# Attention and gated FFN on one core: batch 0 in two token halves, rows of h turned by copies, loads unpaced, targets set anew

## The chip, the cores and the metric

The kernel runs on one core of one Trainium2 chip. The metric is the device time of one execution in microseconds, as the median of several runs; lower is better. The engines are TensorE (PE, with its weight loads as PEld), VectorE (DVE), ScalarE (ACT), GpSimd (POOL) and SyncE (SP), which here only issues DMAs.

## The reference

Eight batches of 576 tokens go through windowed attention (8 heads of 64, window of 32 to each side) and then through a feed-forward layer that is gated by a convolution over three tokens:

```python
scores = scale * np.matmul(q, k.transpose(0, 1, 3, 2))          # q, k, v: (8, 8, 576, 64)
scores = np.where(np.abs(pos[:, None] - pos[None, :]) <= 32, scores, -1e9)
attn = softmax(scores)                                          # + 1e-9 in the denominator
x = np.matmul(attn, v)             # heads side by side: (8, 576, 512)
h = np.maximum(x @ w_in, 0.0)      # (8, 576, 1024)
conv_out = sum(conv_w[k] * hp[:, k:k + S, :] for k in range(3))  # hp: h with a zero row at each end
gate = 1.0 / (1.0 + np.exp(-conv_out))
out = (h * gate) @ w_out           # (8, 576, 512), float32
```

## The kernel before, in words

**A planner writes the order.** The kernel first describes its work as tasks in `Order.add`: the engines that may run the task with a modelled duration (`act`, `dve`, `pl`, `pe`, `dma`), what it reads and writes, the PSUM banks that it opens, and a target `t`. `Order.run` is a list scheduler at build time: of the tasks that are ready on an engine it takes the one with the smallest target, a task that ACT or DVE may do goes to the one that would be done first, and DMAs are modelled as one channel with so many packets of so many ns. The result is a fixed program order on each engine. The targets come from `PARAMS`. All instructions are issued through one helper, so they all carry line 274 in the profile; the trace is read by tiles.

**Attention, for each batch.** `loads` issues on SP four loads of q and k (two head groups; `qst`, `kst`) and five blocks of v (`vst`; 128 tokens with an offset of 32), all float32; POOL casts them to bf16 (`qb`, `kb`, `ve`), and DVE makes `vo`, the blocks of v shifted by 64 partitions. One staging buffer exists for each, and two sets of the cast tiles. `transposes` turns q and k on PE (`qT`, `kT`), `scores` computes 64 x 128 blocks around the diagonal, ACT takes the exponential into `attn`, DVE multiplies by the mask, `values` multiplies by v (with a column of ones for the sum), DVE normalises into `xn`, and `x_turned` turns that into `xT`.

**FFN, in chunks of 384 tokens.** Two batches make three chunks (c 0 to 11). `first` multiplies by `w_in` for each of eight blocks m of 128 rows of h and applies relu into `hT`. `gates` does the convolution on PE by small diagonal matrices of 32 x 32; block m's result comes out turned by 32 x (m mod 4) partitions, so that four matmuls use different parts of the array. Hence h itself has to be turned too, for six of the eight blocks: `moves` does this by DMAs on SP from `hT` to `gT`, two for each shift `s_`. ACT takes a tanh into `tn`, DVE forms the product in place in `gT` (with `hT` directly for the blocks that aren't turned), and `second` multiplies by `w_out`, whose rows were loaded turned to match. ACT or DVE copies the result to `wst`, and SP stores it. c 1 is done in two parts, since its first half needs only batch 0.

**Order at the start.** SP's order is batch 0's q, k and v, then w_in, batch 1's loads, w_out, then the moves, later loads and stores as the planner has them. From batch 2 on, `paced` makes each load wait for the load before the last. As SP works in order, a DMA that waits for its source holds those behind it.

Of the kernel before, what the change touches and what calls it, by code (L numbers as in the profile page):

```python
# [31 lines left out]
class Order:  # L32
# [3 lines left out]
    def __init__(self):  # L36
        self.tasks, self.writer, self.readers = [], {}, {}

    def add(self, kinds, emit, t, reads=(), writes=(), opens=None, ps=(), after=(), claims=()):


        deps = set(after)
        soft = set()
        for k in claims:
            soft.update(self.readers.get(k, ()))
        for k in reads:
            if k in self.writer:
                deps.add(self.writer[k])
        for k in writes:
            if k in self.writer:  # L50
                deps.add(self.writer[k])
            deps.update(self.readers.get(k, ()))
        task = Task(len(self.tasks), kinds, emit, t, deps, opens, ps)
        task.soft = soft - deps
        for k in reads:
            self.readers.setdefault(k, []).append(task)
        for k in writes:
            self.writer[k] = task
            self.readers[k] = []
        for p in ps:  # L60
            p.readers += 1
        self.tasks.append(task)
        return task
# [131 lines left out]
def kernel(  # L195
# [53 lines left out]
    hT_pp = [sb([128, MB, CH + (4 if i == 1 else 2)], BF16, f"hT{i}") for i in range(3)]  # L249
# [98 lines left out]

    def loads(b):
        i = b % NLD  # L350

        def load_qk(y, j):
# [4 lines left out]
            )  # L357

# [21 lines left out]
        if b < 2:  # L380
            x, dx = (-100.0 if b == 0 else -50.0), 0.1
        else:
            x, dx = t0 - PARAMS["LD"], Q["LX"]
# [3 lines left out]
        def paced():  # L387
            return before[-2:-1] if b > 1 and len(before) > 1 else []

        for j in range(NPH):  # L390
            for y in range(2):
                t = x + n * dx
                o.add({"SP": dma(256, 110)}, lambda e, y=y, j=j: load_qk(y, j), t,
                      writes=[("st", y, j)], after=paced())
                before.append(o.tasks[-1])
                o.add({"POOL": pl(1152)}, lambda e, y=y, j=j: cast_qk(y, j, e), t,
                      reads=[("st", y, j)], writes=[("b", i, y, j)])
                n += 1
        for c in range(NBLK):
            t = x + n * dx  # L400
            o.add({"SP": dma(1024, 21)}, lambda e, c=c: load_v(c), t, writes=[("vst", c)], after=paced())
            before.append(o.tasks[-1])
            o.add({"POOL": pl(512)}, lambda e, c=c: cast_v(c, e), t,
                  reads=[("vst", c)], writes=[("ve", i, c)])
            n += 1
        for cs in ((0, 2), (2, 4)) if b == 0 else ((0, 4),):
            for half in range(2):
                o.add({"DVE": dve(520 * (cs[1] - cs[0]), 4)},
                      lambda e, cs=cs, half=half: shift(half, cs), x + n * dx,
                      reads=[("ve", i, c + half) for c in range(*cs)],  # L410
                      writes=[("vo", i, c, half) for c in range(*cs)])

    def load_w_in():
        for h in range(2):
# [9 lines left out]
            o.add({"SP": dma(512, 95)}, load, -60.0, writes=[("ws", 4 * h + c) for c in range(4)])  # L424
            for c in range(KC):
                o.add({"POOL": pl(512)}, lambda e, h=h, c=c: cast(e, h, c), -60.0 + h,
                      reads=[("ws", 4 * h + c)], writes=[("w_in", h, c)])

    def load_w_out():
        rows = moe_w_out.rearrange("(h c p) f -> p h c f", c=4, p=128)  # L430
        for c in range(4):
            def load(e, c=c):
                for lo, at, n in turn(c):
# [5 lines left out]
            o.add({"SP": dma(256, 95, len(turn(c)))}, load, -40.0,  # L439
                  writes=[("ws", 4 * h + c) for h in range(2)])  # L440
            for h in range(2):
                o.add({"POOL": pl(512)}, lambda e, h=h, c=c: copy(e, w_out_sb[:, 4 * h + c, :], ws[:, 4 * h + c, :]),
# [18 lines left out]
    def conv_weights():  # L461
        ps = Banks(1)
        o.add({"PE": pe(200.0, "f32")},
              lambda e: tensor.matmul(bank(ps, 0)[:, 0:3 * MB], conv_w24, ident24, start=True, stop=True),
              5.0, opens=ps, writes=[("cw24",)])
        o.add({"DVE": dve(24)}, lambda e: vector.tensor_copy(
            out=conv_w_sb.rearrange("p k m -> p (k m)"), in_=bank(ps, 0)[:, 0:3 * MB]),
            5.0, reads=[("cw24",)], writes=[("cw",)], ps=[ps])
        o.add({"DVE": dve(768)}, lambda e: vector.tensor_tensor(
# [5 lines left out]
    def transposes(g2):  # L475
# [3 lines left out]
        i, n = b % NLD, g2 % NKT  # L479
        for y in range(2):  # L480
# [16 lines left out]
            o.add({"PE": pe(280.0, "rows")}, mm, t + Q["TR"],  # L497
                  reads=[("b", i, y, j)], writes=[("tr", g2, y)], opens=ps,
                  claims=[("T", n, y, h) for h in range(2)])
            for h in range(2):  # L500
                o.add({"ACT": act(576), "DVE": dve(576)},
                      lambda e, ps=ps, h=h, to=to: copy(
                          e, to[:, h, :, :], half(ps, h).rearrange("p (j x) -> p x j", x=64)),
                      t + Q["TC"], reads=[("tr", g2, y)], writes=[("T", n, y, h)], ps=[ps])
# [4 lines left out]
    def scores(g):  # L509
# [3 lines left out]
        for part, ts in enumerate((range(0, 5), range(5, 9))):  # L513
            ps = Banks(2, 2)
            w = 64 * len(ts)

            def mm(e, ps=ps, ts=ts):
                for x in ts:
# [8 lines left out]
            o.add({"PE": pe(28.0 * len(ts), "rows")}, mm, t + Q["SC"] * d,  # L527
                  reads=[("T", n, y_, y) for y_ in range(2)],
                  writes=[("sc", g, part)], opens=ps, claims=[("a", a, part)])
            o.add({"ACT": act(2 * w)},  # L530
# [3 lines left out]
                  t + Q["EX"] * d, reads=[("sc", g, part)], writes=[("a", a, part)], ps=[ps])  # L534
        o.add({"DVE": (850.0, 850.0, None)},
# [3 lines left out]
    def values(g):  # L539
# [5 lines left out]
        ps = Banks(2, 2)  # L545

        def mm(e):
            for h in range(2):
                for c in range(NBLK):
                    for j in range(2):  # L550
                        x = min(2 * c + j, NT - 1)
                        tensor.matmul(
                            bank(ps, h)[64 * j:64 * j + 64, 65 * c:65 * c + 65],
# [6 lines left out]
        o.add({"PE": pe(29.0 * 10, "cols")}, mm, t + Q["AV"] * d,  # L560
              reads=[("a", a, 0), ("a", a, 1)] + [("ve", i, c) for c in range(NBLK)]
              + [("vo", i, c, h) for c in range(NBLK - 1) for h in range(2)],
              writes=[("av", g)], opens=ps, claims=[("xn", b % 2, pr), ("rec", a)])

        def po():
            return pair(ps, 0)[:, :, 0:65 * NBLK].rearrange("p e (c x) -> p e c x", x=65)

        o.add({"DVE": dve(70)}, lambda e: vector.reciprocal(rec, po()[:, :, :, 64]), t + Q["AX"] * d,
              reads=[("av", g)], writes=[("rec", a)], ps=[ps])
        h0 = head(pr, 0)  # L570
        o.add({"DVE": dve(640)},
              lambda e: vector.tensor_tensor(
                  out=xn_pp[b % 2][:, :, h0:h0 + 3:2, :].rearrange("p c e d -> p e c d"),
                  in0=po()[:, :, :, 0:64],
                  in1=rec[:, :, :, None].broadcast_to([128, 2, NBLK, 64]), op=ALU.mult),
              t + Q["AX"] * d, reads=[("av", g), ("rec", a)], writes=[("xn", b % 2, pr)], ps=[ps])

    def x_turned(b, c, n):

        t, d = pair_t[b * NP + NP - 1]  # L580
        t = t + Q["XT"] * d + 0.1 * c
# [7 lines left out]
        def mm(e):  # L589
            for i in range(n):  # L590
# [7 lines left out]
        o.add({"PE": pe(4 * n * (cols / 2.4 + 3))}, mm, t,  # L598
              reads=[("xn", b % 2, i) for i in range(NP)], writes=[("xps", b, c)], opens=ps,
              claims=[("xT", b // 2 % 2, b % 2, c + i) for i in range(n)])  # L600
        o.add({"ACT": act(4 * n * cols), "DVE": dve(4 * n * cols)},
# [4 lines left out]
              writes=[("xT", b // 2 % 2, b % 2, c + i) for i in range(n)], ps=[ps])  # L606


    def span(c, part):
# [3 lines left out]
        return (lo, hi) if part is None else ((lo, lo + HW + 1), (hi - HW - 1, hi))[part]  # L613

    def first(c, m, part, t):
# [19 lines left out]
        def relu(e):  # L635
# [10 lines left out]
            else:  # L646
                o0 = 1 if kind == 0 else 0
# [3 lines left out]
            else:  # L651
# [3 lines left out]
        o.add({"PE": pe(4 * (n / 2.4 + 3))}, mm, t,  # L655
              reads=need + [("w_in", m // 4, i) for i in range(KC)], writes=[("ph", c, m, part)], opens=ps,
              claims=[("h", kind, m, p_) for p_ in ((0, 1) if part is None else (part,))])
        o.add({"ACT": act(n), "DVE": dve(n)}, relu, t + Q["RL"], reads=[("ph", c, m, part)],
              writes=[("h", kind, m, p_) for p_ in ((0, 1) if part is None else (part,))], ps=[ps])
# [28 lines left out]
    def moves(c, qds, part, t):  # L688
        kind, halves, n, taps, gate = views(c, part)
        for s_ in range(1, 4):  # L690
            ms = [4 * qd + s_ for qd in qds]

            def move(e, m=ms[0], s_=s_):
                for lo, to, cnt in turn(s_):
                    if len(qds) > 1:
                        sync.dma_start(gate(m, to, to + cnt, 2, 4), taps(m, 1, lo, lo + cnt, 2))
                    else:
                        sync.dma_start(gate(m, to, to + cnt), taps(m, 1, lo, lo + cnt))

            runs = 2 if kind == 1 and part is None else 1  # L700
            o.add({"SP": dma(128 * runs * len(qds), 46 if n > HW and runs == 1 else 28, 2, PARAMS["MV"])},
                  move, t, reads=[("h", kind, m, p_) for m in ms for p_ in halves],
                  writes=[("g", c % 3, m, p_) for m in ms for p_ in halves])

    def gates(c, qd, part, t, late):
# [7 lines left out]
        def mm(e):  # L713
            for kk in range(3):
# [8 lines left out]
        o.add({"PE": pe(3 * (n / 2.4) + 100.0, "conv")}, mm, t,  # L723
              reads=[("h", kind, m, p_) for m in ms for p_ in halves] + [("diag",)],
              writes=[("pc", c, qd, part)], opens=ps,
              claims=[("tn", tn_i, u) for u in range(2)])
        for u in range(2):
            o.add({"ACT": act(2 * n)},
                  lambda e, u=u: scalar.activation(
                      tn[:, 2 * u:2 * u + 2, 0:n], pair(ps, 2 * u)[:, :, 0:n], AF.Tanh, bias=0.0, scale=1.0),  # L730
                  t + Q["TN"], reads=[("pc", c, qd, part)], writes=[("tn", tn_i, u)], ps=[ps])
        for m0, count, us in ((0, 1, (0,)), (1, 1, (0,)), (2, 2, (1,))):
            m = 4 * qd + m0
            ii = [("h", kind, m, p_) for p_ in halves] if m0 == 0 else []

            def product(e, m=m, m0=m0, count=count):
# [4 lines left out]
                else:  # L741
# [4 lines left out]
            o.add({"DVE": dve(n * count)}, product, late,  # L746
                  reads=[("tn", tn_i, u) for u in us] + ii,
                  writes=[("g", c % 3, m + x, p_) for x in range(count) for p_ in halves])
# [9 lines left out]
    def second(c, i, t):  # L758
# [4 lines left out]
        def mm(e):  # L763
            for m in range(MB):
# [6 lines left out]
        o.add({"PE": pe(8 * 216.0)}, mm, t,  # L771
              reads=[("g", c % 3, m, p_) for m in range(MB) for p_ in halves]
              + [("w_out", m) for m in range(MB)], writes=[("py", c, i)], opens=ps, claims=[("ws", n)])
# [94 lines left out]
```

## Time and profile before

| what | value |
|---|---|
| median of 3 runs | 242.4 us (242.24 to 243.18) |
| profiled execution | 243.37 us, span from first to last instruction 241.7 us |
| PE busy | 208.1 us (86%) |
| DVE, ACT, POOL busy | 160.1, 164.0, 80.9 us |
| DMA queue of SP | 67152 packets, 49.03 MB, 71.6% of 16 engines |
| mean granted TensorE clock | 0.972 |
| moves of h (gT from hT) | 102 DMAs |

Busy times are those of the whole span; each stage has its own limit. "Granted clock" is the share of TensorE's full clock that the throttle let through. A row of the timeline gives start, duration, engine, operation with output and inputs, a count where like instructions were merged, and in brackets the idle time before it with what ended it. A group's row gives the count, then total busy time and the mean of one in ns.

### The profile page before, as it was taken

To read this page: it belongs to the slowest core of one execution; us is meant where nothing else is said; L and a number is where in the kernel's file an instruction comes from. 1 tells how busy PE (TensorE), PEld (TensorE's weight loads), DVE (VectorE), ACT (ScalarE), POOL (GpSimd) and SP (SyncE) were. 2 spreads that over 40 slices of the span, in tenths; PEclk is the share of its full clock that TensorE was granted. 3 is DMA by queue.
4 is the path that set the end of the run, shared out by engine and by line. 5 is a ranking of instruction groups with operands and counts; after the bars stand their busy time and mean duration, and the time that the engine had idled before them with its cause. 6 is when DMAs were issued, how large, how long until landed. Compare 5 with 4: busy or idle time off the path is not lost. (4 is left out here: it accounts for less than half of the span.)

```text
span 241.7 us, 9128 instructions
## 1 busy us (share of the span) xinstructions
PE 208.1 (86%) x3878; PEld 124.3 (51%) x3906; DVE 160.1 (66%) x268; ACT 164.0 (68%) x291; POOL 80.9 (33%) x96
## 2 busy tenths in 40 slices
PE   1536995589998869999999998999999999999993
PEld 0425464365655454565455654655555655555541
DVE  7586166998575899546399779698684595524140
ACT  1650586445698576679977886679778885876751
POOL 5757744536613444662236517321000000000000
PEclk9999999758999997999999999999999999999999
DMA  6999999989698899969489989756132223342534
GB/s 237 292 289 392 248 233 223 275 229 337 168 290 186 217 293 355 328 186 278 98 207 356 264 225 281 161 129 205 37 129 55 79 105 68 123 110 54 177 113 181
DMA packets 67228, 49.62 MB, mean 205 GB/s; under 512 B 46172, under 2 KB 52340, under 8 KB 67188
## 3 DMA queue, kind: packets, MB, share of 16 engines
q1 hardware_dynamic: 67152, 49.03, 71.6%
q8 instruction: 30, 0.49, 0.9%
q14 instruction: 10, 0.08, 0.1%
q10 hardware_dynamic: 36, 0.01, 0.0%
HBM read 32.52 MB, written 9.44 MB: 174 GB/s over the span
## 5 line engine op out<-in xcount | busy, mean ns | idle before, releaser
L274 PE MATMUL pst<-xT,w_in_sb 128*128 128x385 bf16 (+2 forms) x416 | 75.4, 322 | 1.6 <-ACT xT L274 0.6
L274 PE MATMUL pst<-w_out_sb,gT 128*128 128x512 bf16 x260 | 64.3, 384 | 3.2 <-issue 2.2
L274 PEld LDWEIGHTS <-w_in_sb 128*128 128x128 bf16 x416 | 37.6, 100 | 25.8 <-issue 3.4
L274 ACT ACTIVATE hT<-pst 128x385 bf16<-128x385 f32 (+2 forms) x80 | 38.6, 489 | 11.1 <-PE pst L274 10.1
L274 DVE SCALAR_TENSOR_TENSOR gT<-tn,gT 128x384 bf16<-128x384 f32 (+2 forms) x52 | 42.4, 842 | 3.9 <-DMA gT<-hT 3.9
L274 POOL CAST ve<-vst 128x512 bf16<-128x512 f32 x40 | 29.4, 741 | 45.7 <-DMA vst<-in_v_dram 43.5
L274 ACT ACTIVATE attn<-pst 128x640 bf16<-128x640 f32 x64 | 39.4, 667 | 4.9 <-PE pst L274 4.9
L274 PEld LDWEIGHTS <-gT 128*128 128x128 bf16 x288 | 26.6, 99 | 31.0 <-issue 3.3
L274 ACT ACTIVATE tn<-pst 128x768 f32<-128x768 f32 (+1 forms) x52 | 37.4, 768 | 6.5 <-PE pst L274 4.6
L274 ACT COPY wst<-pst 128x512 f32<-128x512 f32 x36 | 21.2, 588 | 29.6 <-PE pst L274 28.1
L274 DVE TENSOR_TENSOR attn<-attn,mask 128x1152 bf16<-128x1152 bf16 x32 | 26.9, 846 | 12.3 <-ACT attn L274 12.1
L274 DVE TENSOR_TENSOR xn<-pst,rec 128x640 bf16<-128x640 f32 x32 | 25.8, 818 | 0.5
L274 DVE SCALAR_TENSOR_TENSOR gT<-tn,hT 128x384 bf16<-128x384 f32 (+1 forms) x26 | 14.7, 564 | 16.5 <-ACT tn L274 16.4
L274 POOL CAST qb<-qst 128x1152 bf16<-128x1152 f32 x16 | 19.9, 1242 | 16.2 <-DMA qst<-in_q_dram 12.5
L274 POOL CAST kb<-kst 128x1152 bf16<-128x1152 f32 x16 | 19.9, 1243 | 16.0 <-DMA kst<-in_k_dram 14.3
L274 PE MATMUL pst<-hT,diag_w 32*32 32x384 bf16 (+1 forms) x1248 | 21.2, 322 | 1.8 <-DVE xn L274 1.0
L274 ACT COPY xT<-pst 128x1024 bf16<-128x1024 bf16 (+1 forms) x16 | 11.8, 781 | 13.9 <-PE pst L274 13.9
L274 PEld LDWEIGHTS <-attn 128*64 128x64 bf16 x640 | 14.1, 119 | 13.6 <-issue 8.6
L274 PE MATMUL pst<-ve,attn 128*64 128x65 bf16 x384 | 17.4, 206 | 3.8 <-DVE attn L274 2.3
L274 PE MATMUL pst<-qT,kT 64*128 64x64 bf16 x576 | 17.5, 197 | 3.1 <-DVE kT L274 0.8
L274 PE MATMUL pst<-vo,attn 128*64 128x65 bf16 x256 | 15.6, 206 | 3.3 <-DVE vo L274 3.3
L274 PEld LDWEIGHTS <-kT 64*128 64x128 bf16 x576 | 12.2, 98 | 12.0 <-issue 9.2
(37 smaller groups left out, 163.4 us busy)
## 6 DMA issues: line engine op xcount, KB each, us to landing
qst<-in_q_dram SPq DMA_DIRECT2D x16, 576.0 KB, 6.4
kst<-in_k_dram SPq DMA_DIRECT2D x16, 576.0 KB, 7.3
out_dram<-wst SPq DMA_DIRECT2D x11, 768.0 KB, 5.8
vst<-in_v_dram SPq DMA_DIRECT2D x24, 256.0 KB, 5.5
vst<-in_v_dram SPq DMA_DIRECT2D x16, 192.0 KB, 5.9
wst<-in_moe_w_in_dram SPq DMA_DIRECT2D x2, 1024.0 KB, 7.9
gT<-hT SPq DMA_DIRECT2D x14, 144.0 KB, 3.6
gT<-hT SPq DMA_DIRECT2D x34, 48.0 KB, 2.1
```

The lines of the kernel that those rows point to most:

```text
L274: return lambda *args, **kwargs: fixed(do(*args, **kwargs))
```

## The change

- **Batch 0 in halves.** q and k of batch 0 are loaded, cast and transposed for tokens 0 to 287 and then 288 to 575 (`load_half`, `cast_half`, `transposes_half`). Scores, exponential, mask, values and normalisation of batch 0 are split likewise (4 and 5 tiles of 64 tokens; 2 and 3 blocks of 128). `first` does c 0 in two parts of 193 columns, the first with only the first half's tokens; gates and second GEMM of c 0 stay whole. The order of the early loads on SP is fixed by a chain (`line=lead`): first half of q and k, v blocks 0 to 2, w_in's first half, second half of q and k, v blocks 3 and 4, w_in's second half, batch 1, w_out.
- **Copies for moves.** A shift by 32 or 96 partitions is four copies of 32 partitions, by 64 two of 64, on DVE or ACT as the planner picks. `hT` gets two more columns and starts one element later, so that the unshifted tap lies on an even element.
- **Loads unpaced.** `paced` returns nothing.
- **w_in's casts** may go to ACT as well as POOL; the planner books half as much for DVE's copies of xT.
- **Targets.** `PARAMS` has new values, and a table `NUDGE` adds an offset to the target of each kind of task, by batch or chunk.

```diff
-    hT_pp = [sb([128, MB, CH + (4 if i == 1 else 2)], BF16, f"hT{i}") for i in range(3)]
+    hT_pp = [sb([128, MB, CH + (6 if i == 1 else 4)], BF16, f"hT{i}")[:, :, 1:] for i in range(3)]
...
+        def load_half(y, j, half):
+            src = (q, k)[y][b, 4 * j:4 * j + 4, 32 * RP * half:32 * RP * half + 32 * RP, :]
+            sync.dma_start(
+                qkst[y][j][:, half, :, :].rearrange("p j d -> p (j d)"),
+                bass.AP(src.tensor, src.offset, [[S * D, 4], [RP * D, 32], [1, RP * D]]),
+            )
...
         def paced():
-            return before[-2:-1] if b > 1 and len(before) > 1 else []
+            return []
...
+        if b == 0:
+            for half in range(2):
+                t = x + 3.0 * half
+                for j in range(NPH):
+                    for y in range(2):
+                        o.add("qk", {"SP": dma(128, 110)}, lambda e, y=y, j=j, half=half: load_half(y, j, half),
+                              t, writes=[("st0", y, j, half)], sub=half, line=lead)
...
+                for c in (range(0, 3), range(3, NBLK))[half]:
+                    v_block(c, t)
+                    t += 0.1
+                v_shift((2 * half, 2 * half + 2), t)
+                load_w_in(half, t + 1.0)
+            return
...
+    def transposes_half(g2, y, half, t):
+        j, n = g2 % NPH, g2 % NKT
+        to = (qT_pp[n], kT_pp[n][:, :, PAD:PAD + S])[y].rearrange("p y (x j) -> p y x j", j=RP)
+        ps = Banks(1)
...
+        def mm(e):
+            for x in range(RP):
+                for h in range(2):
+                    rows = slice(64 * h, 64 * h + 64)
+                    tensor.transpose(turned()[rows, x, :], half_of(y, j, half)[rows, x, :], ident[rows, rows])
...
         for s_ in range(1, 4):
             ms = [4 * qd + s_ for qd in qds]
-
-            def move(e, m=ms[0], s_=s_):
-                for lo, to, cnt in turn(s_):
+            wide = 64 if s_ == 2 else 32
+            for lo in range(0, 128, wide):
+                to = (lo + 32 * s_) % 128
+
+                def move(e, m=ms[0], lo=lo, to=to, wide=wide):
                     if len(qds) > 1:
-                        sync.dma_start(gate(m, to, to + cnt, 2, 4), taps(m, 1, lo, lo + cnt, 2))
+                        copy(e, gate(m, to, to + wide, 2, 4), taps(m, 1, lo, lo + wide, 2))
                     else:
-                        sync.dma_start(gate(m, to, to + cnt), taps(m, 1, lo, lo + cnt))
-
-            runs = 2 if kind == 1 and part is None else 1
-            o.add({"SP": dma(128 * runs * len(qds), 46 if n > HW and runs == 1 else 28, 2, PARAMS["MV"])},
-                  move, t, reads=[("h", kind, m, p_) for m in ms for p_ in halves],
-                  writes=[("g", c % 3, m, p_) for m in ms for p_ in halves])
+                        copy(e, gate(m, to, to + wide), taps(m, 1, lo, lo + wide))
+
+                o.add("mv", {"DVE": dve(n * len(qds), 4), "ACT": act(n * len(qds))},
+                      move, t + PARAMS["MV"], reads=[("h", kind, m, p_) for m in ms for p_ in halves],
+                      writes=[("gm", c % 3, m, p_, to + x) for m in ms for p_ in halves for x in range(0, wide, 32)],
+                      sub=s_ - 1 + 4 * (ms[0] // 4) + 8 * int(c == 1 and part == 0))
...
+        if c == 0:
+            for m in range(MB):
+                first(c, m, 0, T0 + Q["A0"] + m * 0.5)
         for part, t, dt in parts:
             single = c == NCH - 1 or (c % 3 == 1 and part is None)
             for qd in range(2):
                 for m in range(4 * qd, 4 * qd + 4):
-                    first(c, m, part, t + m * dt)
+                    first(c, m, part if c else 1, t + m * dt)
...
-PARAMS = {"P": 23.98, "T0": 17.65, "T1": 35.65, "T2": 7.73, "B1": 27.27, "LD": 15, "LEAD": 0,
+PARAMS = {"P": 26.5, "T0": 10, "T1": 34.66, "T2": 16, "B1": 22.98, "LD": 21.05, "LEAD": 6.54,
...
+NUDGE = {
+    "qk": {0: 63.75, 1: -13.56, 2: 10.14, 3: -27.5, 4: 36.59, 5: 72.93, 6: -35.27, 7: 8.81,
...
```

240 lines of the change are left out of this document (159 added, 81 removed), and 79 rows, old and new, of tables (NUDGE, PARAMS).

## The prediction

> **What bounds the kernel now.** I read the page's totals first, then the busy time by stretch, then the queues of the first stretch in order of time, last the waits behind it.
>
> ```profile
> span 241.7 us, 9128 instructions
> ...
> PE 208.1 (86%) x3878; PEld 124.3 (51%) x3906; DVE 160.1 (66%) x268; ACT 164.0 (68%) x291; POOL 80.9 (33%) x96
> ```
>
> PE is busy for 208.1 of 241.7 us. The 33.6 us without PE work, and the time that PE ran at a reduced clock, are what a reordering can win. The stretches show where they lie (columns: stretch, its length, busy time of PE, PEld, DVE, ACT, POOL with instruction counts, then granted clock, DMA share, GB/s).
>
> ```profile
> 0.00:25.00 25.00, 10.83 (x246) 8.83 (x246) 17.36 (x43) 9.20 (x14) 16.90 (x27) 1.00 1.01 305
> 25.00:45.00 20.00, 15.77 (x344) 10.46 (x344) 11.06 (x20) 13.66 (x25) 11.52 (x17) 1.00 0.99 222
> 45.00:50.00 5.00, 2.23 (x53) 1.63 (x48) 4.71 (x10) 0.60 (x1) 1.53 (x2) 0.54 0.88 277
> 50.00:55.00 5.00, 5.00 (x123) 3.57 (x122) 4.43 (x8) 3.07 (x5) 2.29 (x2) 0.50 0.89 280
> 60.00:100.00 40.00, 35.34 (x715) 21.69 (x717) 30.09 (x45) 30.01 (x55) 18.54 (x20) 0.96 0.92 259
> 60.00:160.00 100.00, 92.95 (x1850) 55.33 (x1862) 73.78 (x114) 77.57 (x140) 43.14 (x46) 0.98 0.88 243
> 60.00:242.00 182.00, 169.40 (x3067) 97.01 (x3091) 117.82 (x184) 134.80 (x240) 45.72 (x49) 0.99 0.64 182
> ```
>
> PE idles 14.2 us in the first 25, 4.2 in the next 20, 2.8 from 45 to 50, and 4.7 from 60 to 100. After 100 it is nearly solid. From 45 to 55 the granted clock is about half: at full clock the 2.23 and 5.00 us of work would have taken about 2.23 x 0.46 + 5.00 x 0.50 = 3.5 us less; from 60 to 100, 35.34 x 0.04 = 1.4 us less. Through the first 45 us the DMA engines are full (share 1.01 and 0.99), so there the order of the bytes decides when PE can work. In order of time, first SP's issues, then POOL's casts, then PE's first work on w_in and w_out:
>
> ```profile
> 0.80 0.44 SPq L274 DMA_DIRECT2D qst<-in_q_dram  x1
> ...
> 34.58 8.04 SPq L274 DMA_DIRECT2D gT<-hT  x6
> 42.72 0.55 SPq L274 DMA_DIRECT2D qst<-in_q_dram  x1
> ```
>
> ```profile
> 16.49 0.99 POOL L274 CAST ve<-vst 128x512 bf16<-128x512 f32 x1 [0.56 <-DMA vst<-in_v_dram]
> ...
> 34.57 0.62 POOL L274 CAST ve<-vst 128x512 bf16<-128x512 f32 x1 [1.53 <-DMA vst<-in_v_dram]
> ...
> 42.11 1.64 POOL L274 CAST w_out_sb<-wst 128x512 bf16<-128x512 f32 x2 [1.39 <-DMA wst<-in_moe_w_out_dram]
> ```
>
> ```profile
> 25.54 4.12 PE L274 MATMUL pst<-xT,w_in_sb 128*128 128x385 bf16 x16 [0.55 <-ACT xT L274]
> ...
> 34.83 0.85 PE L274 MATMUL pst<-xT,w_in_sb 128*128 128x193 bf16 x8
> ...
> 54.62 2.37 PE L274 MATMUL pst<-w_out_sb,gT 128*128 128x512 bf16 x7
> ```
>
> Batch 0's last v block is there at 16.49, and PE's first feed-forward matmul starts 9.0 us later, at 25.54. Batch 1's last v block is there only at 34.57. SP then spends 8.04 us on six moves of h, whose sources it waits for, and batch 2's first load stands behind them until 42.72. w_out is cast by 43.75, but PE touches it first at 54.62, because c 0's products come late:
>
> ```profile
> 49.64 3.70 DVE L274 SCALAR_TENSOR_TENSOR gT<-tn,gT 128x384 bf16<-128x384 f32 x4
> ```
>
> **The change, part by part.** *Batch 0 in halves.* The first FFN matmuls of c 0 (32 of 193 columns) need only 256 tokens. At 226 KB/us (batch 0's 3.54 MB in the 15.7 us from SP's first issue at 0.80 to 16.49), the first half's 1.90 MB (four half loads of q and k, three blocks of v) are there near 9.2 us. The chain behind its v was 9.0 us for all tokens; for half I take 7, which gives 16.2 us. w_in's first half, 1.05 MB and next in the queue, comes 3.4 us later at the stretch's 305 GB/s, near 12.6, and is cast by then, on POOL or now ACT. So up to 32 matmuls x 0.85/8 = 3.4 us of PE work move from behind 25.54 into idle time. Against it, the second half's q, k and v now stand behind that w_in half and land 2 to 4 us later than 16.49, and with them the rest of c 0 and the half chunk of c 1. Bounds 0 and -3.4; I take **-2.0**. The price in work: transposes of batch 0 double (72 more), four more mask products, reciprocals and normalisations each, eight more relus. All lie before 30 us, where PE idles 14 us and DVE 7.6; I cost them at nothing. If that cover is gone, the transposes cost about 2.6 us (72 at 0.66 us for 18):
>
> ```profile
> 5.96 0.66 PE L274 MATMUL pst<-ident,qb 64*128 64x64 bf16 x18 [2.14 <-POOL qb L274]
> ```
>
> *45 to 55 us.* PE waits here for batch 1's masks and normalised rows while c 0's last GEMM, 24 matmuls, lies unusable behind moves and products. After the change a move is a copy queued directly behind its relus, so c 0's products can run near 38 to 42 instead of 49.64, and the GEMM can start when w_out is cast, 43.75. The page has such matmuls at 64.3 us for 260:
>
> ```profile
> L274 PE MATMUL pst<-w_out_sb,gT 128*128 128x512 bf16 x260 | 64.3, 384 | 3.2 <-issue 2.2
> ```
>
> That is 0.25 us each and 5.9 us for the 24, enough to cover the 2.8 idle and to keep the clock up. Bounds 0 and -(2.8 + 3.5) = -6.3; I take **-5.0**, since DVE is itself nearly full there (4.71 and 4.43 of 5) and now carries copies too. Late next is DVE's attention chain for batch 1.
>
> *60 to 100 us.* Loads no longer stand behind moves in SP's queue:
>
> ```profile
> L274 SPq DMA_DIRECT2D gT<-hT x102: 496/627/1922, 34.6 to 230.2; - x102
> ```
>
> 102 issues at a median of 627 ns leave SP, 64 us of its queue, and 6.9 MB of small transfers leave the DMA engines. Nothing is moved ahead of the loads but other loads and output stores. Idle plus reduced clock here is 4.7 + 1.4 = 6.1. PE's waits after 60 us name engines rather than loads:
>
> ```profile
> PE pst L274 <- DVE xn L274: 2.3, 4, 1.0
> ...
> PE pst L274 <- ACT attn L274: 0.8, 4, 0.3
> PE pst L274 <- ACT qT L274: 0.7, 2, 0.5
> PE pst L274 <- DVE vo L274: 0.7, 1, 0.7
> ```
>
> But xn, qT and vo are late because their batch arrived late, at least in part. Bounds 0 and -6.1; I take **-3.0**, half.
>
> *The copies.* Each chunk's 6 row blocks become 10 copies per group: 70 copies of 768 elements (seven chunks) and 100 of 384 (c 1 in two parts, c 4, 7, 10, 11 in two quads each), 170 in all. The nearest operation is the vo copy, SBUF to SBUF in bf16 across partitions:
>
> ```profile
> 13.77 0.43 DVE L274 COPY vo<-ve 64x1040 bf16<-64x1040 bf16 x1
> ...
> 90.90 1.59 DVE L274 COPY vo<-ve 64x2080 bf16<-64x2080 bf16 x1
> ...
> 95.73 0.69 DVE L274 COPY vo<-ve 64x2080 bf16<-64x2080 bf16 x1
> ```
>
> ```profile
> 90.80 1.15 POOL L274 CAST qb<-qst 128x1152 bf16<-128x1152 f32 x1 [0.73 <-DMA qst<-in_q_dram]
> ```
>
> From 0.43 and 0.69: 0.17 us + 0.25 ns an element, so 0.36 us for 768 and 0.27 for 384, 52 us if all run on DVE. ACT's copy from PSUM bounds it from above, 1.02 us for 1024 elements, some 0.8 for 768:
>
> ```profile
> L274 ACT COPY xT<-pst 128x1024 bf16<-128x1024 bf16 x10 | 10.1, 1017 | 13.7 <-PE pst L274 13.7
> ```
>
> I take DVE's, as the planner picks the engine that is done first. After 60 us there are 60 wide and 90 narrow ones: 45.9 us. DVE and ACT together go from 117.8 + 134.8 = 252.6 to 298.5 of 2 x 181.7, from 70% to 82%; the free share falls from 30.5% to 17.9%. If PE's waits for them (2.3 + 0.8 + 0.7 + 0.7 = 4.5) grow as the free share shrinks, by 1.7, that is **+3.2**. Behind a copy on its engine stand the next relu, mask or product, and PE waits for those. Bounds: 0 if the copies lie in slack, +9.2 in the second rival.
>
> The vo copies also show what POOL does to them: 0.69 us alone, 1.59 when the copy began 0.1 us after a POOL cast of 1.15 us did. The Trainium skill, SBUF — State Buffer, "Who interferes with whom", says that a DVE copy in a two-port mode and a GpSimd instruction exclude each other, the second waiting for the whole of the first. The two rows bear it out, and it speaks against the change, which puts copies where transfers did not meet POOL at all; by it the sum would be that of the second rival, 247.1, where all the waiting counts.
>
> *Targets.* They reorder each queue's ready work. No row shows their worth; they are in the range, at 0.
>
> The sum: -2.0 - 5.0 - 3.0 + 3.2 = -6.8. The span goes from 241.7 to 234.9; the profiled execution took 243.37 (1.7 around its span), 0.4% above the median of 242.4. From the median: **235.6 us**.
>
> **The rivals.** *Everything lands.* -3.4 - 6.3 - 6.1 + 1.6 (half the charge): 228.2. For it: PE's solid stretch after 100 starts as early as data allow. Against: it needs batch 1 sooner than 34.57, and those bytes are no fewer.
>
> *DVE becomes the bound, slower.* POOL is busy 43 of the 100 us from 60 to 160. A copy meets a cast with a chance of 0.43 and waits half of the 0.9 seen: 0.19 more each, 28 us over 150 copies. DVE and ACT would be 327 of 363, 90% full; the free share is a third, and 4.5 us of waits become 13.7: +9.2. Then the 60 to 100 gain is gone and half of that at 45: 242.4 - 2.0 - 2.5 + 9.2 = 247.1. It decides from a mean copy above 0.5 us. The planner books 265 and 165 ns, so its order would come apart there. For it: the 1.59 and 4 products in 3.70 us at 49.64. Against: after 160 POOL is idle, and ACT can take copies.
>
> *Nothing changes.* Batch 1's data rule the start: first term 0, second half (-3.2), third 0, copies +3.2: 242.4.
>
> **How the numbers follow.** This kernel can be told from no change at about 0.5%, 241.2 to 243.6. Chances: forecast 0.54 (its own range 231 to 240), everything lands 0.16, nothing changes 0.08, DVE the bound 0.22. So faster 0.70, same 0.08, slower 0.22. Leaving out about half of each outer case, the range is 229 to 246.5.
>
> **What would show it.** Right: PE's first w_in matmul near 16.2 us; w_out matmuls from about 44; granted clock near 1.0 from 45 to 55; DVE's copies of h at 0.27 to 0.36 us; busy DVE plus ACT about 50 us up. Wrong: PE waiting for gT or hT after 100 us, copies over 0.5 us on average, PE idle from 60 to 160 above 12 us, or batch 0's second half so late that PE idles from 25 to 45 more than the 4.2 us of now.

## The result, and the profile after

The change made the kernel slower: 274.25 us (median of four, 270.86 to 275.77) against 242.79 us, a ratio of 1.1215 with a 95% interval of 1.1083 to 1.1347, or about 29 us. I had forecast 235.6 us. One of the four runs of before took 341.61 us, and two of after, the profiled one of 275.77 us among them, lie over 1.5% above the fastest: the ratios, here and below, leave such runs out, the medians do not, and stages are compared with that difference in mind.

First the page's totals, then the busy time by stretch (the columns are those of the tables above).

```profile
span 274.0 us, 9232 instructions
...
PE 218.5 (80%) x4010; PEld 130.0 (47%) x4010; DVE 215.2 (79%) x426; ACT 183.7 (67%) x327; POOL 79.1 (29%) x96
...
L283 DVE COPY gT<-hT 32x384 bf16<-32x384 bf16 (+3 forms) x126 | 45.2, 359 | 3.7 <-ACT hT L283 1.1
L283 ACT COPY gT<-hT 32x384 bf16<-32x384 bf16 (+3 forms) x44 | 28.8, 655 | 4.5 <-DVE hT L283 3.6
```

```profile
0.00:25.00 25.00, 7.01 (x146) 5.37 (x146) 9.16 (x37) 7.05 (x11) 8.04 (x18) 1.00 0.44 135
25.00:45.00 20.00, 13.11 (x222) 10.77 (x222) 7.53 (x19) 7.67 (x16) 9.15 (x12) 0.69 0.79 250
45.00:60.00 15.00, 10.52 (x221) 8.01 (x217) 11.59 (x27) 11.73 (x24) 7.80 (x12) 0.96 1.11 255
60.00:100.00 40.00, 28.55 (x676) 17.48 (x676) 37.89 (x61) 24.32 (x48) 20.32 (x20) 0.83 1.01 260
100.00:160.00 60.00, 53.76 (x996) 30.34 (x995) 54.53 (x98) 46.30 (x81) 19.94 (x20) 0.97 0.68 184
160.00:220.00 60.00, 55.85 (x1085) 32.49 (x1054) 56.30 (x105) 47.38 (x84) 13.80 (x16) 1.00 0.27 81
```

Of before, the stretches that were not shown yet:

```profile
45.00:60.00 15.00, 12.12 (x231) 8.01 (x228) 13.90 (x24) 6.39 (x12) 6.74 (x7) 0.66 0.96 295
...
100.00:160.00 60.00, 57.62 (x1147) 33.64 (x1149) 43.70 (x69) 47.56 (x86) 24.60 (x26) 1.00 0.85 232
```

Two things stand out. In the first 25 us the DMA engines, which were full before (1.01), are used to 0.44, and PE does 7.01 us in place of 10.83. And DVE is nearly full from 60 us on: 37.89 of 40 and 54.53 of 60, where it had been 30.09 and 43.70. PE's busy time weighted with the granted clock, summed to 160 us, is 126.1 us before (10.83 + 15.77 + 12.12 x 0.66 + 35.34 x 0.96 + 57.62) and 102.0 after. By this estimate 24 of the 32 us of longer span are lost before 160, in work that PE could have done and did not; of the rest a part is that loads and casts come later (POOL is busy 13.80 us after 160, where it was 2.58 in the same 60 us).

### The profile page after: what moved, and what is told of

It is laid out like the page before. It is cut to its first block, busy times and chain, and to the rows that moved or that the text cites. A ratio compares the mean times of both kernels' runs of the same rounds, so it can differ in the third digit from the quotient of the medians.

```text
span 274.0 us, 9232 instructions
## 1 busy us (share of the span) xinstructions
PE 218.5 (80%) x4010; PEld 130.0 (47%) x4010; DVE 215.2 (79%) x426; ACT 183.7 (67%) x327; POOL 79.1 (29%) x96
## 4 chain that ended last, share of the span: by engine, by line
PE 43%; DVE 35%; SPq 6%; DMA 6%; issue 4%; ACT 4%; POOL 0%; DVEq 0%; ACTq 0%
PE pst L283 43%; DVE gT L283 17%; SPq L283 6%; DMA kst<-in_k_dram 6%; DVE vo L283 4%; DVE xn L283 3%; DVE attn L283 3%; DVE hT L283 3%; DVE xT L283 2%; DVE qT L283 1%; ACT tn L283 1%; ACT attn L283 1%; ACT hT L283 1%; DVE rec L283 1%; DVE kT L283 1%
## 5 line engine op out<-in xcount | busy, mean ns | idle before, releaser
L283 PE MATMUL pst<-xT,w_in_sb 128*128 128x385 bf16 (+3 forms) x448 | 77.0, 319 | 2.7 <-DVE hT L283 2.4
L283 DVE COPY gT<-hT 32x384 bf16<-32x384 bf16 (+3 forms) x126 | 45.2, 359 | 3.7 <-ACT hT L283 1.1
L283 ACT ACTIVATE hT<-pst 128x385 bf16<-128x385 f32 (+3 forms) x77 | 34.4, 460 | 14.4 <-PE pst L283 13.6
L283 ACT ACTIVATE attn<-pst 128x640 bf16<-128x640 f32 (+1 forms) x64 | 38.8, 654 | 5.3 <-PE pst L283 4.9
L283 DVE TENSOR_TENSOR attn<-attn,mask 128x1152 bf16<-128x1152 bf16 (+2 forms) x36 | 26.6, 747 | 14.2 <-ACT attn L283 13.7
L283 ACT COPY gT<-hT 32x384 bf16<-32x384 bf16 (+3 forms) x44 | 28.8, 655 | 4.5 <-DVE hT L283 3.6
L283 POOL CAST kb<-kst 128x1152 bf16<-128x1152 f32 (+1 forms) x18 | 21.1, 1172 | 20.2 <-DMA kst<-in_k_dram 18.6
L283 DVE TENSOR_TENSOR xn<-pst,rec 128x640 bf16<-128x640 f32 (+2 forms) x36 | 26.2, 742 | 0.6
L283 POOL CAST qb<-qst 128x1152 bf16<-128x1152 f32 (+1 forms) x18 | 19.5, 1082 | 24.3 <-DMA qst<-in_q_dram 23.8
L283 DVE TENSOR_SCALAR hT<-pst 128x385 bf16<-128x385 f32 (+3 forms) x35 | 16.8, 480 | 6.8 <-PE pst L283 5.8
```

The costliest lines, as they stand in the source:

```text
L283: return lambda *args, **kwargs: fixed(do(*args, **kwargs))
```

## The experiments

The times are medians; the ratio to the kernel before, run on the same chip, stands behind them. 1% is 2.4 us.

**1. The form of the half loads.** `e1_spread` issues each half load as four DMAs of 32 partitions, with the same program order on all compute engines:

```diff
-            src = (q, k)[y][b, 4 * j:4 * j + 4, ...]
-            sync.dma_start(qkst[y][j][:, half, :, :]..., bass.AP(src.tensor, src.offset, [[S * D, 4], [RP * D, 32], [1, RP * D]]))
+            for r in range(4):
+                src = (q, k)[y][b, 4 * j + r, ...]
+                sync.dma_start(qkst[y][j][32 * r:32 * r + 32, half, :, :]..., bass.AP(src.tensor, src.offset, [[RP * D, 32], [1, RP * D]]))
```

> The changed kernel in the same order on every engine, but each half load of q and k of batch 0 is sent as four DMAs of 32 partitions instead of one whose source has four heads as its slowest dimension. Theory A (the eight half loads run on few DMA engines, 3.1 us each one after the other, and hold the start up): casts of the four first halves done by about 9 us instead of 17, first w_in matmul near 18 instead of 26.3, time down by 8 to 15 us, to 259 to 266. Theory B (DVE is the bound through the copies, the start hardly counts): the start is earlier, but the time falls by less than 4 us, to 270 or more. Theory C (the targets make a poor order on the chip): less than 4 us too.

Measured: 264.27 us, 1.096 (1.0874 to 1.1046). Against after that is 10.0 us by medians, 6.2 by the ratios: theory A's 8 to 15 us are met by the one and missed by the other, and theory B's 4 are passed by both. In the changed kernel POOL's casts, in order of time, show when each half load lands:

```profile
7.08 0.66 POOL L283 CAST qb<-qst 128x576 bf16<-128x576 f32 x1 [3.97 <-DMA qst<-in_q_dram]
10.20 0.67 POOL L283 CAST kb<-kst 128x576 bf16<-128x576 f32 x1 [2.45 <-DMA kst<-in_k_dram]
13.45 0.67 POOL L283 CAST qb<-qst 128x576 bf16<-128x576 f32 x1 [2.58 <-DMA qst<-in_q_dram]
16.23 0.80 POOL L283 CAST kb<-kst 128x576 bf16<-128x576 f32 x1 [2.11 <-DMA kst<-in_k_dram]
```

One load of 128 x 576 float32, 295 KB, lands each 3.05 us ((16.23 - 7.08) / 3), 97 GB/s; and while only such loads are under way, the stretch of after shows 0.26 of the 16 DMA engines in use:

```profile
4.00:7.00 3.00, 0.00 (x0) 0.00 (x0) 1.68 (x11) 0.00 (x0) 0.00 (x0) 1.00 0.26 101
```

In the same 3 us, the whole loads of before use all of them:

```profile
4.00:7.00 3.00, 0.66 (x18) 0.50 (x18) 2.71 (x12) 1.63 (x2) 1.95 (x2) 1.00 1.02 378
```

0.26 of 16 is about four engines. The half load's slowest dimension is the four heads of a group. With four pieces of 32 partitions each, the same casts stand closer (the first and the last of the four, of `e1_spread`):

```profile
4.29 0.66 POOL L283 CAST qb<-qst 128x576 bf16<-128x576 f32 x1 [1.18 <-DMA qst<-in_q_dram]
...
9.78 0.67 POOL L283 CAST kb<-kst 128x576 bf16<-128x576 f32 x1 [1.07 <-DMA kst<-in_k_dram]
```

**2. The copies left out.** `e2_nocopy` and `e3_spread_nocopy` are after and `e1_spread` with the copies' bodies empty; the turned rows of `gT` are zeros, so the output lacks h there.

```diff
+    for t_ in gT_pp:
+        vector.memset(t_, 0.0)
...
                 def move(e, m=ms[0], lo=lo, to=to, wide=wide):
-                    copy(...)
+                    return
```

> The changed kernel in the same order, with all 170 copies of h left out (gT is zeroed once at the start, so the gated rows of six of eight blocks are zero); loads as in the changed kernel. Theory A: the copies cost little beyond what the start costs, down by at most 8 us, 266 to 272. Theory B: DVE loses 45 us of work and ACT 29, PE idles less after 45 us, down by 15 to 25 us, to 250 to 259. Theory C: down by less than 6 us, since the order makes PE wait for other things.

> Both edits: half loads in four pieces, and the copies left out. If start and copies explain the loss between them, this comes to 236 to 246, about the kernel before or better. Theory C: it stays above 252, because the order itself is poor.

Measured: 256.25 us, 1.0598 (1.0527 to 1.0669), and 249.84 us, 1.0294 (1.0207 to 1.0381). By the ratios the copies cost 14.9 us in the one and 16.1 in the other (18.0 and 14.4 by medians), and the form of the loads costs 7.3 without copies too (6.4 by medians). Neither suspect explains the other. The zeroing hardly moves the start here (first w_in matmul at 26.2 and 22.2 us, with copies 26.28 and 21.75). And `e3_spread_nocopy`, which has neither copies nor moves nor pacing, is still 3% slower than before, between the two times that were expected of it. So the 29 us of the changed kernel split into some 15 for the copies, 7 for the form of the loads and 7 that both edits leave.

**3. The copies alone, in the kernel before.** `e4_before_copies` keeps batch 0 whole, the pacing and the targets, and replaces only the moves (`hT` lies one element later, as in the change, and the order is planned anew):

```diff
-            o.add({"SP": dma(...)}, move, ...)                        # sync.dma_start of turn(s_)
+            for lo in range(0, 128, wide):
+                o.add({"DVE": dve(n * len(qds), 4), "ACT": act(n * len(qds))}, move, ...)   # copy(e, gate(...), taps(...))
```

> The kernel before, with its own targets, batch 0 whole and paced loads, and only the 102 moves replaced by the 170 copies on DVE or ACT (planned anew with the copies' modelled costs, each copy targeted right behind its relus). Theory A: within 5 us of the kernel before, 238 to 247. Theory B: the copies alone cost 10 to 20 us, 252 to 262.

Measured: 264.26 us, 1.0932 (1.0861 to 1.1002). So the copies alone, with the order planned around them, cost 22 us, more than either theory had. The stretches and the groups of copies of this kernel:

```profile
45.00:60.00 15.00, 6.47 (x134) 3.88 (x134) 14.81 (x24) 5.52 (x12) 10.58 (x9) 0.50 0.78 250
60.00:100.00 40.00, 32.23 (x705) 20.51 (x708) 34.17 (x61) 27.98 (x54) 12.56 (x15) 0.94 0.75 191
100.00:160.00 60.00, 52.36 (x934) 31.10 (x942) 53.34 (x91) 48.49 (x84) 27.31 (x27) 0.94 0.71 193
160.00:220.00 60.00, 57.70 (x1047) 32.70 (x1054) 50.33 (x99) 51.33 (x90) 3.38 (x6) 1.00 0.17 58
60.00:262.00 202.00, 180.62 (x3188) 104.19 (x3213) 163.12 (x309) 160.03 (x282) 43.25 (x46) 0.97 0.45 128
```

From 45 to 60 PE does 6.47 us at half clock, in place of 12.12 at 0.66; from 60 to 100 it loses 3.1, and from 100 to 160 it loses 5.3 more, at 0.94. Weighted with the clock as above, 4.8 us are lost in the first of these stretches, 3.6 in the second and 8.4 in the third (6.47 x 0.50, 32.23 x 0.94 and 52.36 x 0.94 against before's 8.0, 33.9 and 57.6). After 160 PE is full again (57.70 of 60), though nearly half of DVE's copies (57 of 119) run after 180 us: there they are almost free. And the same copy has three prices in three stretches. DVE's copies of 32 x 384 of this kernel from 40 to 60, from 60 to 160, and from 180 to the end, when POOL has no casts left (each row is from the groups of one such window):

```profile
L274 DVE COPY gT<-hT 32x384 bf16<-32x384 bf16 x4 | 2.4, 606 | 0.1
...
L274 DVE COPY gT<-hT 32x384 bf16<-32x384 bf16 x15 | 6.0, 403 | 0.3
...
L274 DVE COPY gT<-hT 32x384 bf16<-32x384 bf16 x33 | 8.3, 252 | 6.7 <-ACT hT L274 6.2
```

These means mix two kinds. Of all 52 such copies on DVE, 44 overlap no POOL instruction, and each takes 248 to 256 ns; eight overlap casts, and they take 257 to 1206 ns, 712 on the mean. The one of 1206 began at 79.13, just behind a cast that ran from 79.08 to 80.23, and ended 0.1 us after it. How it reaches PE is seen in the timeline near 50 us: first POOL, then DVE, then PE of `e4_before_copies`.

```profile
45.60 1.47 POOL L274 CAST qb<-qst 128x1152 bf16<-128x1152 f32 x1
47.02 1.47 POOL L274 CAST kb<-kst 128x1152 bf16<-128x1152 f32 x1
48.43 1.86 POOL L274 CAST qb<-qst 128x1152 bf16<-128x1152 f32 x1
```

```profile
45.98 3.31 DVE L274 SCALAR_TENSOR_TENSOR gT<-tn,gT 128x384 bf16<-128x384 f32 x2
49.21 0.35 DVE L274 TENSOR_SCALAR hT<-pst 128x193 bf16<-128x193 f32 x1
49.59 0.81 DVE L274 COPY gT<-hT 32x384 bf16<-32x384 bf16 x1
50.44 0.76 DVE L274 TENSOR_TENSOR attn<-attn,mask 128x1152 bf16<-128x1152 bf16 x1
51.22 3.10 DVE L274 COPY gT<-hT 64x384 bf16<-64x384 bf16 x5
54.34 0.76 DVE L274 TENSOR_TENSOR attn<-attn,mask 128x1152 bf16<-128x1152 bf16 x1
```

```profile
49.61 0.85 PE L274 MATMUL pst<-qT,kT 64*128 64x64 bf16 x25 [3.63 <-DVE hT L274]
...
55.15 0.26 PE L274 MATMUL pst<-ve,attn 128*64 128x65 bf16 x1 [2.39 <-DVE attn L274]
```

While POOL casts back to back, two products of 384 take 3.31 us, though they are no copies, PE waits 3.63 us for the relu behind them, and a copy takes 0.81. Five copies, 3.10 us, stand between a mask product and the next, and PE waits 2.39 us for that next one. How much of the 22 us comes from such meetings with casts, and how much from the copies' undisturbed time, was not separated: no run has the copies without the casts.

**4. Time of the copies, or the order that the planner made of them?** `e5_copies_booked` is `e4_before_copies` with DVE's copies booked nearer to what they take, `e6_copies_pool` gives all of them to POOL:

```diff
-    {"DVE": dve(n * len(qds), 4), "ACT": act(n * len(qds))}
+    {"DVE": (240 + 0.25 * n * len(qds), 300 + 0.25 * n * len(qds), None), "ACT": act(n * len(qds))}    # e5
+    {"POOL": pl(n * len(qds))}                                                                        # e6
```

> The kernel before with the copies, as in the fourth experiment, but the planner books a copy on DVE at 0.24 us + 0.25 ns an element (0.43 and 0.34 us, what the traces show with the waiting for POOL) in place of 0.265 and 0.165, so more copies go to ACT and the order allows for them. Theory B1 (the copies' time itself fills DVE): the time stays within 5 us of the fourth experiment, 259 to 269. Theory B2 (the order comes apart because copies are booked too cheap): 246 to 255.

> The kernel before with the copies, all 170 on POOL, which is busy for a third of the span before. Theory B1 (DVE's time is what counts): DVE is back near 160 us busy and the time comes to 240 to 252. Rival (POOL's longer work shuts DVE out of the port that both use, and delays the casts of the loads): 255 or more.

Measured: 255.82 us, 1.0606 (1.0533 to 1.0678), and 280.99 us, 1.1621 (1.1541 to 1.1702). Booking nearer to the truth wins back 8.4 us, 0.8 short of what theory B2 asked: ACT takes 77 copies, not 51, and PE gets 10.36 us of work in 45 to 60. On POOL the copies take 821 ns in the median, and DVE waits for them; the page of `e6_copies_pool`, and its waits (time in total, how often, the longest):

```profile
PE 221.5 (80%) x3906; PEld 128.4 (46%) x3906; DVE 179.2 (64%) x271; ACT 164.8 (59%) x288; POOL 217.8 (78%) x266
```

```profile
DVE gT L274 <- POOL gT L274: 19.2, 13, 3.2
```

`e9_before_copies_left_out` has the engine order of `e4_before_copies` without the copies, `e10_before_moves_left_out` that of before without the moves (in both, `gT`'s turned rows are zeros).

> The fourth experiment (kernel before with copies, 264 us) in the same order on every engine, with the copies left out (gT zeroed once, so the gated rows of six of eight blocks are zero). If the copies' own time on DVE and ACT, with their waiting for POOL, makes the loss of 22 us, 238 to 246. If the order that the planner makes around them is the larger part, 250 or more.

> The kernel before in the same order, with its 102 moves by DMA left out (gT zeroed once, gated rows of six of eight blocks are zero). The prediction's view that moves hold back loads and products by some 5 to 8 us: 233 to 238. Rival (the moves were hidden already): 239 to 244.

Measured: 251.86 us, 1.0412 (1.0352 to 1.0471), and 251.35 us, 1.0393 (1.0314 to 1.0472). Both were spoiled by the zeroing itself, which stood at the start on DVE and pushed the first w_in matmul from 25.5 to 30.3 and 30.6 us. I moved it to DVE's idle time near 25 us, in `e13_e9_late_zero` and `e14_e10_late_zero`:

> The ninth experiment again (kernel before with copies, in that order, copies left out), but gT is zeroed on DVE at about 25 us, where DVE is idle, instead of at the start, where the three zeroings of 1.6 us held up batch 0 and put the first w_in matmul at 30.3 instead of 25.5. If the copies' own time makes the loss: 243 to 248. If the order around them does: 250 or more.

> The tenth experiment again (kernel before in its order, moves by DMA left out), with gT zeroed at about 25 us instead of at the start. If moves by DMA were hidden already: 239 to 244. If they held the kernel back as the prediction had it: 233 to 238.

Measured: 245.63 us, 1.0118 (1.0044 to 1.0192), and 245.07 us, 1.0132 (1.0072 to 1.0191). `e13_e9_late_zero` and `e4_before_copies` differ by the copies' own time (and the zeroing): 18.6 us by medians, 19.7 by ratios, so about that much of the 22 is time on the engines, and 3 to 4 are the order when no copy stands in it. That is no contradiction to `e5_copies_booked`: which engine takes the copies, and when, decides how much of their time is lost, and 8 us of it can be had back. The stretches of `e13_e9_late_zero` show PE's work back:

```profile
45.00:60.00 15.00, 13.54 (x237) 6.98 (x236) 13.33 (x19) 7.42 (x14) 10.80 (x10) 0.77 0.89 279
...
100.00:160.00 60.00, 57.85 (x1109) 33.35 (x1109) 51.04 (x79) 44.31 (x78) 23.13 (x25) 1.00 0.58 157
```

And in `e14_e10_late_zero` the moves are gone at no engine's cost but the zeroing's, and the kernel is no faster than before: the 102 DMAs that the change removes were hidden. The zeroing puts DVE's next copy at 31.20 us instead of 30.16, 1.0 us later; a gain of 5 to 8 us could be hidden by it only if it cost 8 us or more, and no row suggests that.

**5. The other parts.** `e8_after_whole` is after with batch 0 whole (`if b == 0` branches out); copies, unpaced loads, targets and ACT's casts of w_in stay. `e7_after_dma_moves` is `e1_spread` with moves as DMAs on SP again. `e11_before_unpaced` is before with `paced` returning nothing. `e12_early_copies` is before with copies for c 0 and the first part of c 1 only. `e15_spread_booked` is `e1_spread` with the booking of `e5_copies_booked`. `e16_before_p` is before with `P` at 24.48 in place of 23.98, a new plan and nothing else.

> The changed kernel with batch 0 whole again (loads, attention and c 0 as before the change), copies, unpaced loads and targets kept. If the half loads were the only thing wrong with the halves, this equals the run with the half loads in four pieces, 260 to 268. If the halves cost by themselves even when their loads are quick (72 more transposes, more small instructions, w_in behind them), 254 to 260. If the targets need the halves, 268 or more.

> The changed kernel with half loads in four pieces, and the 102 moves by DMA back in place of the copies (planned anew, other targets as in the change). If the copies are the larger cause and moves by DMA are nearly free, 247 to 254, as with the copies left out. Rival (without pacing, moves and loads now get in each other's way on SP): 257 or more.

> The kernel before with one edit: loads from batch 2 on no longer wait for the load before the last (planned anew). If loads sent earlier help by themselves, as the prediction's third term has it, 236 to 241. If they hold up the moves on SP or run into buffers that are not free, 244 to 255. If it is nothing, 241 to 244.

> The kernel before with copies only for c 0 and the first half of c 1 (20 copies), all later moves by DMA. The prediction's second term (products of c 0 earlier, PE fed from 45 to 55 us, clock kept up): 236 to 240. Rival (DVE is full from 40 to 60 us, and copies that wait for POOL's casts there delay batch 1's masks and rows): 243 to 250.

> The changed kernel with half loads in four pieces and copies on DVE booked at 0.43 and 0.34 us, as the fifth experiment had it for the kernel before. If too cheap booking is a part of the loss there as well, 254 to 260 (from 264). If the new targets carry only the order that they were set for, 263 or more.

> The kernel before with a single target parameter moved by 2% (the pace P from 23.98 to 24.48), which reorders about as many instructions as unpacing the loads does. If an order without set targets costs some 7 us whatever the edit, 247 to 252. If the unpaced loads and the early copies cost by what they do, 241 to 245 here.

| kernel | us | ratio (95%) |
|---|---|---|
| e8_after_whole | 264.41 | 1.0951 (1.0862 to 1.1040) |
| e7_after_dma_moves | 261.25 | 1.0839 (1.0746 to 1.0933) |
| e11_before_unpaced | 249.61 | 1.0344 (1.0238 to 1.0449) |
| e12_early_copies | 249.99 | 1.0323 (1.0250 to 1.0396) |
| e15_spread_booked | 264.07 | 1.0823 (1.0753 to 1.0892) |
| e16_before_p | 244.39 | 1.0115 (1.0042 to 1.0188) |

`e8_after_whole` closes the account: before with copies 1.0932, with unpaced loads and the new targets on top 1.0951, with halves whose loads are spread 1.0960, with the half loads as the change has them 1.1215. In this sequence the halves, the unpaced loads and the targets together come to nothing beside the copies; they need not be nothing each, as `e11_before_unpaced` alone costs 3.4%. `e16_before_p` shows that one new plan alone costs about 1%. If the new plan of `e12_early_copies` costs as much, its 3.2% is some 5 us for its 20 copies, a quarter of the loss for an eighth of the copies: 14 of them ran on DVE, at 521 ns.

`e7_after_dma_moves` stays 8% slow for another reason: with the changed plan SP waits in order for moves, which the waits of its queue show (30.8 us for `hT` from ACT, where before has 19.4). What of its 8% is this and what is targets made for another kernel, I did not separate.

```profile
SPq L283 <- ACT hT L283: 30.8, 14, 9.8
```

`e11_before_unpaced` says that pacing was worth some 3%, of which a new plan may be 1; through what, I did not follow beyond its waits, where PE now waits 7.5 us for `xn` (5.2 before). In the changed kernel the nearer booking brings 0 (by medians) to 3 us (by ratios, whose intervals overlap), not 8; why less than in before is open.

## Why the prediction was wrong, point by point

**The copies (+3.2 forecast; measured about +22 in the kernel before, about +15 in the changed one) are the term that failed most.** The fill came out close: DVE and ACT were to be 82% full after 60 us, and in `e4_before_copies` they are 163.12 + 160.03 of 404, 80%. The cost in engine time was too low, and the way from fill to lost time was wrong:

- I took 0.27 and 0.36 us from copies of v that met no cast and put all copies on DVE: 52 us. That is what undisturbed copies on DVE take (0.25 and 0.35 us). But in `e4_before_copies` they took 44.3 us for 119 on DVE and 32.0 for 51 on ACT, 76 us. At the undisturbed durations on DVE the same 170 copies would be 50 us; of the 26 us more, some 17 are ACT's longer copies (509 and 829 ns), and 9 come from DVE copies that met POOL's casts.
- I scaled PE's waits of 4.5 us by the free share of two engines averaged over 180 us. But PE's waits are for masks, `xn` and products, which DVE alone makes, in the part before 160, where DVE was at 13.90 of 15 from 45 to 60 already and went from 43.70 to 53.34 of 60 from 100 to 160. Of DVE's 119 copies 47 start between 40 and 160 us, and 57 behind 180, where PE loses nothing. PE's waits for DVE's `xn`, `hT`, `vo` and `attn` in after are 11.9 + 6.2 + 2.8 + 2.7 = 23.6 us, where before had 5.2 + 3.3 + 2.3 = 10.8; its waits for POOL's casts of q and k grew by as much, from 3.3 to 16.6 us, 10.6 of them in the first 25 us, the late start below:

```profile
PE pst L283 <- DVE xn L283: 11.9, 7, 4.2
PE pst L283 <- POOL qb L283: 9.8, 4, 4.0
PE pst L283 <- POOL kb L283: 6.8, 3, 2.7
PE pst L283 <- DVE hT L283: 6.2, 10, 1.1
...
PE pst L283 <- DVE vo L283: 2.8, 3, 1.5
PE pst L283 <- DVE attn L283: 2.7, 4, 1.6
```

The same waits before:

```profile
PE pst L274 <- DVE xn L274: 5.2, 7, 1.1
...
PE pst L274 <- DVE vo L274: 3.3, 4, 1.7
...
PE pst L274 <- DVE attn L274: 2.3, 3, 1.0
...
PE pst L274 <- POOL qb L274: 2.1, 1, 2.1
```

- The rival "DVE becomes the bound" had the mechanism, and the rule it rested on holds: the Trainium skill, SBUF — State Buffer, "Who interferes with whom", has such a copy and a GpSimd instruction shut each other out, and the 252, 403 and 606 ns above agree. It had the price wrong (247.1) and so had its point of decision: a mean copy above 0.5 us. The mean was 359 ns in after and 372 in `e4_before_copies`, and DVE decided all the same: the work that PE loses in `e4_before_copies` lies in all three stretches from 45 to 160 (4.8, 3.6 and 8.4 us), and all of it is back in `e13_e9_late_zero`, without the copies.

**The first term (-2.0 forecast) had the wrong sign.** I costed the half loads by their bytes, at 226 KB/us, and did not look at what their access pattern does to the number of engines. The first half's last q or k block was cast at 16.23 us in place of near 9; the first w_in matmul was due near 16.2 and came at 26.28, later than the 25.54 of before. Only 16 of the 32 matmuls that I had counted could come then, as w_in's first half serves four of the eight blocks; the other 16 came at 40.49:

```profile
26.28 2.77 PE L283 MATMUL pst<-xT,w_in_sb 128*128 128x193 bf16 x16
...
40.49 1.45 PE L283 MATMUL pst<-xT,w_in_sb 128*128 128x193 bf16 x8
```

A rule that I had not weighed bears on it: the Trainium skill, DMA: Bandwidth & Descriptors, "Why a DMA increments its semaphore by 16 and not by 1", lets a transfer use the largest number of engines, up to 16, that divides the slowest dimension of both sides; four heads give four. The trace agrees, with 0.26 of the engines. The form of the loads cost 6 to 7 us by the ratios. But the term would have failed without that: with the loads spread the first w_in matmul comes at 21.75 us and the DMA engines are used to 0.64 in the first 25, which I put down to 16 small issues for each half, not separated from the rest; and `e1_spread` is no faster than `e8_after_whole`. What I had called late by "2 to 4 us", the second half, is late enough to eat the gain, and behind it in the queue stands w_in's second half, which the sum forgot. Before, its casts end at 23.92 us; in after they begin at 38.52, and in `e1_spread` the other 16 matmuls wait for them until 33.22 (the casts of before, then of after, then PE of `e1_spread`):

```profile
21.63 2.29 POOL L274 CAST w_in_sb<-wst 128x512 bf16<-128x512 f32 x4 [0.44 <-DMA wst<-in_moe_w_in_dram]
```

```profile
38.52 1.70 POOL L283 CAST w_in_sb<-wst 128x512 bf16<-128x512 f32 x2 [1.83 <-DMA wst<-in_moe_w_in_dram]
```

```profile
33.22 1.67 PE L283 MATMUL pst<-xT,w_in_sb 128*128 128x193 bf16 x8 [2.10 <-ACT w_in_sb L283]
```

**The second term (-5.0) found c 0 late and its resource taken.** In the changed kernel c 0's own copies begin at 55.18 us, behind the late start, and the first w_out matmul comes at 70.58, against 54.62 before and about 44 in the forecast. The resource I had named myself: DVE is full there, at 4.71 and 4.43 of 5. The clock came as forecast, 0.96 from 45 to 60, but PE does 10.52 us there, not 12.12, and the stretches of low clock only moved, to 25 to 45 (0.69) and 60 to 100 (0.83). Early copies alone (`e12_early_copies`), where c 0 is not late, make the stretch worse: DVE is busy 14.84 of 15 us, the first w_out matmul is at 54.30, and PE does 8.83 us at a granted clock of 0.54.

**The third term (-3.0) had nothing to win.** I read 102 issues at 627 ns as 64 us that loads wait for. `e14_e10_late_zero` takes them away and gives 245.07 us, and `e3_spread_nocopy`, which has the halves, takes the pacing away as well and gives 249.84. The loads behind the moves were not what PE waited for, as the waits shown in the prediction (for `xn`, `attn`, `qT`, `vo`) said; I argued that away with "in part".

**What was right:** the mechanism of the second rival, the remark that POOL's idleness after 160 makes copies cheap there, the targets (no gain seen), and three of the signs of being wrong: PE waits 3.1 us for `hT` after 100 us, it idles 17.7 us from 60 to 160, where 12 was the mark, and 6.9 from 25 to 45, where 4.2 was.

## What to carry to other kernels

Work that moves from the DMA engines to a compute engine must be priced in the stage where it lands, on the one engine that it delays, at the duration that it has there; an average fill over the span hides it. Before asking what a removed transfer gives back, leave it out: if the time stays, it was hidden. When a load is cut, look at its slowest dimension first: halving the bytes also cut its engines to a quarter. And follow what is queued behind it: here the second half of the weights landed some 10 us later than before even with quick loads.

## What the runs showed of the hardware

- A bf16 copy of 32 x 384 on DVE took 252 ns when POOL was idle, 403 on the mean beside some casts and 606 among dense ones, and the eight of `e4_before_copies` that overlapped a cast took 712 on the mean; a copy of 64 partitions cost no more than one of 32 (255 ns for 64 x 384, in the same late stretch as the 252).
- On POOL the copies of h took 821 ns in the median, and DVE waited 19.2 us for them: 280.99 us, the slowest of all. POOL was busy 217.8 us there, and what the later casts cost was not separated.
- A load with four as its slowest dimension ran at 97 GB/s and used 0.26 of the DMA engines.
